# Attention and MLP in one program: turned weights regrouped within SBUF instead of through DRAM, turning placed behind scaling, and the first two MLP blocks spread up to slot 42

## Chip, cores and metric

One core of a Trainium2 chip. The metric is the device time of one execution in microseconds (us). Before the change the median was 1513.23 us of 3 runs (1508.47 to 1516.01).

## The reference

Thresholded attention over 8 batches and 8 heads, then an MLP with exact Gelu on the 4608 tokens that come out of it. All is float32.

```python
batch, n_heads, seq, head_dim = (8, 8, 576, 64)
scores = scale * np.matmul(q, k.transpose(0, 1, 3, 2))
thresh = np.max(scores, axis=-1, keepdims=True) - tau
scores = np.where(scores >= thresh, scores, -1000000000.0)
scores = scores - np.max(scores, axis=-1, keepdims=True)
attn = np.exp(scores)
attn = attn / (np.sum(attn, axis=-1, keepdims=True) + 1e-09)
x = np.matmul(attn, v)                    # (B,H,S,D), bridged to (B*S, H*D) = (4608, 512)
h = x @ w_in                              # d_ff = 2048
g = 0.5 * h * (1.0 + erf(h / sqrt(2)))
out = g @ w_out
```

## The kernel before

The program works on 32 head pairs (two heads of a batch), each in 5 slots: four of 128 queries and a tail of 64. Four pairs are a batch of 576 tokens. The first batch (slots 0 to 19) turns its attention weights with TensorE, while VectorE also converts the MLP weights. From the second batch on, VectorE turns blocks of 32x32 into `pd`, one buffer for each head, and DMA regroups `pd` into `pT`, the layout in which TensorE weighs `v`. `fill` strews MLP matmuls between the slots so that TensorE is never short of work. A block is the MLP of 256 tokens; a piece is one of 32 parts of the MLP weights, each converted by four VectorE instructions. A run is a stretch of contiguous bytes within a transfer; a transfer is issued when the queue takes it up and lands when its last byte is there.

```python
    pd = [const.tile([P, 4 * KR, P], FP32, name=f"pd{e}") for e in range(2)]        # one buffer for each head
    pd_tail = [const.tile([P, 4 * KR, Q], FP32, name=f"pd_tail{i}") for i in range(2)]
# ... cut ...
    def softmax_tail(p, i, early):
        # ... cut: masking (scalar_tensor_tensor on VectorE, reads the scores in PSUM), reciprocal ...
        for e in range(n):
            row = w[:, e * S:(e + 1) * S]
            if early:
                nc.scalar.activation(row, row, AF.Copy, bias=0.0, scale=rden[:, e:e + 1])
            else:
                nc.vector.tensor_scalar(row, row, rden[:, e:e + 1], None, op0=ALU.mult)

    def turn_p(p, i):
        s = st[p]
        w = s.pop(("p", i))
        n = 1 if i == NC else 2
        for e in range(n):
            to = pd_tail[p % 2] if i == NC else pd[e][:, :, i * Q:(i + 1) * Q]
            nc.vector.transpose(to[:, 0:NB, :], w[:, e * S:(e + 1) * S].rearrange("p (b i) -> p b i", i=Q))
        if i == NC - 1:
            s["turned"] = dram.tile([2, Q, 4 * KR, S], FP32, tag="turned", name="turned")
            for e in range(2):
                for a in range(4):
                    nc.sync.dma_start(s["turned"][e, :, :, a * P:(a + 1) * P], pd[e][a * Q:(a + 1) * Q])
        # ... cut: the tail, 4 transfers likewise from pd_tail ...

    def fetch_p(p):
        s = st[p]
        turned = s.pop("turned")
        s["pT"] = [one.tile([P, KR, S], FP32, tag=f"pT{e}", name=f"pT{e}") for e in range(2)]
        for e in range(2):
            nc.sync.dma_start(s["pT"][e], turned[e].rearrange("j (r k) s -> (j r) k s", k=KR))

    def weigh_v(p, h):
        # ... cut: 10 matmuls pT x v for one half (288 columns) of the queries, then ScalarE copies into x_blk ...

# ... cut ...
    for n in range(len(slots) + WEIGH + 1):          # a slot is 128 queries of both heads; slot 4 is the tail of 64
        p, i = divmod(n, SLOTS)
        batch = p // HP
        if p < NP:
            scores(p, i)                             # TensorE
            softmax_head(p, i)                       # row maxima on VectorE, Exp on ScalarE
        if 0 < p <= HP and i == 1:
            weigh_v(p - 1, 1)
            weighed = p
            if p == HP:
                convert(1e12)
                fill(BLK_NS / 2, 1)                  # half of the first MLP block
        if 0 < n <= len(slots):
            (turn_p if n > BATCH else turn_p_early)(*slots[n - 1])     # the slot before, ahead of masking
        if i == 0 and p > HP:
            fetch_p(p - 1)
        if p < NP:
            softmax_tail(p, i, batch < 2)
        # ... cut: loads, turning of q and k, weight conversion, fill() with MLP work ...
        if 0 < p <= HP and i == 0:
            weigh_v(p - 1, 0)
        elif p > HP and i == WEIGH:                  # WEIGH = 3
            for h in range(2):
                weigh_v(p - 1, h)
            weighed = p
```

## Time and profile before

| | before |
|---|---|
| time, median of 3 | 1513.23 us |
| TensorE busy, of the profiled 1511.5 us | 1440.8 us (95%) |
| VectorE busy | 901.7 us (60%) |
| scaling on ScalarE (second batch and first) | 72 instructions of 0.77 us mean |
| HBM traffic | 144.4 MB read, 92.0 MB written |

### The profile page before, as it was taken

Reading aid. Unit: us, or ns where it says so; the run is one execution under the profiler, and the core shown is the slowest. Engines: PE = TensorE matmul, PEld = TensorE weight load, DVE = VectorE, ACT = ScalarE, POOL = GpSimd, SP = SyncE. Lnnn points to the kernel's source line nnn. Section 1 sums busy time; section 2 is a strip of 40 time slices with the busy share of each in tenths; the row PEclk is TensorE's granted clock in tenths of the full one; section 3 lists DMA queues with packets and bytes.
Section 4 is the critical chain, followed back from the end, with each engine's and each line's share of the span. In section 5 each row is a group of like instructions: output and inputs, shape, how many; then the busy total and the mean of one; then the engine's idle time right before and its main releaser. Section 6 shows DMA issues by size and latency. Waiting matters only on the chain.

```text
span 1511.5 us, 17425 instructions
## 1 busy us (share of the span) xinstructions
PE 1440.8 (95%) x6092; PEld 897.7 (59%) x6092; DVE 901.7 (60%) x2089; ACT 635.4 (42%) x928; POOL 41.6 (3%) x84
## 2 busy tenths in 40 slices
PE   5877878899999999999999999999999999999998
PEld 4544635556565656666565656565757474765764
DVE  6998576676666766766766776666676675000000
ACT  5766344744444443535352535353535262110110
POOL 3221100000000000000000000000000000000000
PEclk9798989899999999999999999999999999999999
DMA  9876267767666667685767776666666655400000
GB/s 284 245 219 204 103 167 197 188 172 190 176 153 172 168 169 187 164 207 136 184 175 194 180 183 181 183 180 158 168 162 179 176 150 146 132 14 7 7 14 14
DMA packets 398887, 237.61 MB, mean 157 GB/s; under 512 B 230352, under 2 KB 380880, under 8 KB 391632
## 3 DMA queue, kind: packets, MB, share of 16 engines
q1 hardware_dynamic: 391632, 202.96, 52.1%
q0 software_dynamic: 7168, 33.54, 6.5%
q8 instruction: 49, 0.80, 0.2%
q14 instruction: 38, 0.31, 0.1%
HBM read 144.43 MB, written 92.01 MB: 156 GB/s over the span
## 4 chain that ended last, share of the span: by engine, by line
PE 83%; DVE 9%; ACT 3%; DMA 2%; SPq 2%; issue 1%; ACTq 0%; DVEq 0%
PE o_ps L437 32%; PE hT L426 31%; PE sc L320 11%; PE xT L398 9%; DVE p L345 3%; DVE nmx L331 2%; DVE power L174 1%; DMA turned<-pd 1%; ACT p L332 1%; DVE expo L165 1%; DVE w_in L176 1%; SPq L228 1%; DVE mant L172 1%; DMA pd<-in_moe_w_out_dram 1%; SPq L224 1%
## 5 line engine op out<-in xcount | busy, mean ns | idle before, releaser
L426 PE MATMUL hT<-x,w_in 128*128 128x256 f32 x2304 | 523.8, 385 | 4.0 <-ACT g L430 4.0
L437 PE MATMUL o_ps<-w_out,g 128*128 128x512 f32 x1152 | 516.1, 599 | 0.0
L426 PEld LDWEIGHTS hT<-x,w_in 128*128 128x128 f32 x2304 | 437.4, 192 | 92.2 <-issue 26.7
L331 DVE TENSOR_REDUCE nmx<-sc 128x1 f32<-128x576 f32 x288 | 206.3, 753 | 310.4 <-PE sc L320 309.5
L437 PEld LDWEIGHTS o_ps<-w_out,g 128*128 128x128 f32 x1152 | 215.1, 190 | 260.1 <-issue 257.1
L332 ACT ACTIVATE p<-sc,nmx 128x576 f32<-128x576 f32 x288 | 202.6, 741 | 335.2 <-DVE nmx L331 334.8
L345 DVE SCALAR_TENSOR_TENSOR p<-sc,thr,p 128x576 f32<-128x576 f32 x288 | 220.3, 797 | 14.0 <-ACT p L332 12.8
L320 PE MATMUL sc<-kT,qT 64*128 64x288 f32 x1024 | 185.7, 448 | 34.1 <-DVE p L345 33.6
L320 PEld LDWEIGHTS sc<-kT,qT 64*128 64x128 f32 x1024 | 102.8, 194 | 121.5 <-issue 103.8
L368 DVE STREAM_TRANSPOSE pd<-p 128x576 f32<-128x576 f32 x224 | 162.3, 757 | 14.2 <-DMA turned<-pd 14.1
L398 PE MATMUL xT<-pT,v 128*64 128x288 f32 x1280 | 164.9, 412 | 0.0
L430 ACT ACTIVATE g<-hT 128x512 f32<-128x512 f32 x144 | 85.2, 597 | 138.4 <-PE hT L426 137.7
L398 PEld LDWEIGHTS xT<-pT,v 128*64 128x64 f32 x1280 | 89.4, 138 | 75.3 <-issue 18.5
L356 DVE TENSOR_SCALAR p<-p,rden 128x576 f32<-128x576 f32 x216 | 103.7, 518 | 4.2
L430 ACT ACT_TABLE_LOAD x72 | 92.4, 1283 | 12.6 <-PE hT L426 11.6
L407 ACT COPY x<-xT 128x256 f32<-128x256 f32 (+7 forms) x128 | 29.3, 283 | 150.2 <-PE xT L398 150.2
L332 ACT ACT_TABLE_LOAD x71 | 91.1, 1283 | 2.8 <-DVE nmx L331 1.5
L440 ACT COPY o_sb<-o_ps 128x512 f32<-128x512 f32 x36 | 21.0, 584 | 147.6 <-PE o_ps L437 147.6
L354 ACT ACTIVATE p<-p,rden 128x576 f32<-128x576 f32 x72 | 52.3, 768 | 60.0 <-DVE rden L350 59.5
L320 PE MATMUL sc<-kT,q_tail 128*128 128x288 f32 x128 | 43.1, 462 | 18.7 <-DVE p L345 18.7
L320 PEld LDWEIGHTS sc<-kT,q_tail 128*128 128x128 f32 x128 | 23.3, 202 | 36.3 <-issue 32.4
L335 DVE TENSOR_SCALAR thr<-nmx,tau_eff 128x2 f32<-128x2 f32 (+1 forms) x160 | 36.2, 226 | 5.7
(65 smaller groups left out, 423.3 us busy)
## 6 DMA issues: line engine op xcount, KB each, us to landing
pT<-turned SPq DMA_DIRECT2D x56, 1440.0 KB, 8.1
turned<-pd SPq DMA_DIRECT2D x224, 320.0 KB, 5.2
out_dram<-o_sb SPq DMA_DIRECT2D x36, 256.0 KB, 2.2
turned<-pd_tail SPq DMA_DIRECT2D x112, 80.0 KB, 2.9
q<-in_q_dram SPq DMA_DIRECT2D x112, 72.0 KB, 8.9
k<-in_k_dram SPq DMA_DIRECT2D x112, 72.0 KB, 3.1
v<-in_v_dram SPq DMA_DIRECT2D x168, 40.0 KB, 2.2
raw<-in_moe_w_in_dram POOLq DMA_DIRECT2D x8, 512.0 KB, 7.9
```

The source lines that it names most:

```text
L320: nc.tensor.matmul(sc[e][:, h, 0:HALF], lhsT=lhsT, rhs=s["kT"][rows, at:at + HALF], start=True, stop=True)
L331: nc.vector.tensor_reduce(nmx[:, e:e + 1], sc, axis=AXIS.XY, op=ALU.max, negate=True)
L332: nc.scalar.activation(w[:, e * S:(e + 1) * S].rearrange("p (h s) -> p h s", h=2), sc, AF.Exp, bias=nmx[:, e:e + 1], scale=1.0)
L335: nc.vector.tensor_scalar(thr[:, 0:n], nmx[:, 0:n], -1.0, tau_eff, op0=ALU.mult, op1=ALU.subtract)
L345: nc.vector.scalar_tensor_tensor(row, sc[e][:, :, 0:HALF], thr[:, e:e + 1], row, op0=ALU.is_ge, op1=ALU.mult, accum_out=den[:, e:e + 1])
L354: nc.scalar.activation(row, row, AF.Copy, bias=0.0, scale=rden[:, e:e + 1])
L356: nc.vector.tensor_scalar(row, row, rden[:, e:e + 1], None, op0=ALU.mult)
L368: nc.vector.transpose(to[:, 0:NB, :], w[:, e * S:(e + 1) * S].rearrange("p (b i) -> p b i", i=Q))
L398: nc.tensor.matmul(xT[f, 0:HALF], lhsT=s["v"][:, e, c, :], rhs=pT[:, c, cols], start=(c == 0), stop=(c == KR - 1))
L426: nc.tensor.matmul(hT[:, j % 2, :], lhsT=w_in_sb[c][:, j * P:(j + 1) * P], rhs=x_blk[n][:, c, :], start=(c == 0), stop=(c == N_DM - 1))
L430: nc.scalar.activation(t, hT, AF.Gelu)
L437: nc.tensor.matmul(o[:, 0:d_model], lhsT=g[j][:, m * P:(m + 1) * P], rhs=w_out_sb[j], start=(j == 0), stop=(j == N_DF - 1))
```

## The change

Its intent: the regrouping goes straight from `pd` to `pT`, without the way through DRAM and the 56 reads back. Turning of a slot comes behind its own scaling, not ahead of the masking of the next slot, and scaling moves to VectorE one batch earlier. Two MLP blocks are spread evenly up to slot 42, with the first half of the first between the last weight conversions. For that, the weighing of the first batch is cut unevenly (columns 0 to 256 at slot 2 of the same pair, 256 to 576 at slot 0 of the next). Cut to its core:

```diff
-    dram = ctx.enter_context(tc.tile_pool(name="dram", bufs=2, space=bass.MemoryType.DRAM))
...
-    EARLY_PIECES = 24
+    EARLY_PIECES = 22
...
-            nc.gpsimd.memset(t, 0.0)
+            nc.gpsimd.memset(t[:, :, NB - 3 * KR:KR, :], 0.0)
...
         if i == NC - 1:
-            s["turned"] = dram.tile([2, Q, 4 * KR, S], FP32, tag="turned", name="turned")
+            s["pT"] = [one.tile([P, KR, S], FP32, tag=f"pT{e}", name=f"pT{e}") for e in range(2)]
             for e in range(2):
                 for a in range(4):
-                    nc.sync.dma_start(s["turned"][e, :, :, a * P:(a + 1) * P], pd[e][a * Q:(a + 1) * Q])
+                    regroup(s["pT"][e], a * P, P, pd[e], a)
...   (the tail likewise; fetch_p goes)
+    def regroup(to, at, n, src, a):
+        nc.sync.dma_start(to[:, :, at:at + n], src[a * Q:(a + 1) * Q])
 
-    def weigh_v(p, h):
+    def weigh_v(p, lo, hi):
...   (columns lo to hi in place of a half)
-    WEIGH = 3
-
-    goal = [0.0] + [1.5 + 2.08 * i for i in range(B - 1)]
+    WEIGH = 2
+    FIRST = BLK_NS / 2
+    SECOND = 2 * BLK_NS - FIRST
+
+    goal = [0.0] + [1.9 + 2.03 * i for i in range(B - 1)]
...
+        early = batch == 0
...
-        if 0 < p <= HP and i == 1:
-            weigh_v(p - 1, 1)
-            weighed = p
+        if 0 < p <= HP and i == 0:
+            turn_p_early(p - 1, NC)
+            weigh_v(p - 1, TOK, S)
             if p == HP:
-                convert(1e12)
-                fill(BLK_NS / 2, 1)
-        if 0 < n <= len(slots):
-            (turn_p if n > BATCH else turn_p_early)(*slots[n - 1])
-        if i == 0 and p > HP:
-            fetch_p(p - 1)
+                tokens = S
+        if early and i:
+            turn_p_early(p, i - 1)
         if p < NP:
-            softmax_tail(p, i, batch < 2)
+            softmax_tail(p, i, early)
+        if n == BATCH:
+            for _ in range(len(pieces) - EARLY_PIECES):
+                convert(2100)
+                fill(FIRST / (len(pieces) - EARLY_PIECES), tokens)
+            convert(1e12)
+        if HP <= p < NP:
+            turn_p(p, i)
...
+            if n <= 2 * BATCH + WEIGH:
+                share = SECOND / (BATCH + WEIGH)
+            fill(share, tokens)
+        if early and i == 2:
+            weigh_v(p, 0, TOK)
+            if p == HP - 1:
+                tokens = TOK
         elif p > HP and i == WEIGH:
             for h in range(2):
-                weigh_v(p - 1, h)
-            weighed = p
+                weigh_v(p - 1, h * HALF, (h + 1) * HALF)
+            if p % HP == 0:
+                tokens = batch * S
```

More of the change, by code (lines that the diff above doesn't have):

```diff
@@ L376, in turn_p @@
                 e, at = divmod(a * Q, TAIL)
-                nc.sync.dma_start(
-                    s["turned"][e, :, :, MAIN + at:MAIN + at + Q], pd_tail[p % 2][a * Q:(a + 1) * Q])
-    def fetch_p(p):
-        s = st[p]
-        turned = s.pop("turned")
-        s["pT"] = [one.tile([P, KR, S], FP32, tag=f"pT{e}", name=f"pT{e}") for e in range(2)]
-        for e in range(2):
-            nc.sync.dma_start(s["pT"][e], turned[e].rearrange("j (r k) s -> (j r) k s", k=KR))
-    def weigh_v(p, h):
+                regroup(s["pT"][e], MAIN + at, Q, pd_tail[p % 2], a)
+    def regroup(to, at, n, src, a):
+        nc.sync.dma_start(to[:, :, at:at + n], src[a * Q:(a + 1) * Q])
+    def weigh_v(p, lo, hi):
         b, hp = divmod(p, HP)
         s = st[p]
-        cols = slice(h * HALF, (h + 1) * HALF)
         xT = ps.tile([P, 512], FP32, tag="mm", name="xT")
@@ L398, in weigh_v @@
                 nc.tensor.matmul(
-                    xT[f, 0:HALF], lhsT=s["v"][:, e, c, :], rhs=pT[:, c, cols],
+                    xT[f, 0:hi - lo], lhsT=s["v"][:, e, c, :], rhs=pT[:, c, lo:hi],
                     start=(c == 0), stop=(c == KR - 1))
-        at = lo = b * S + h * HALF
-        while at < lo + HALF:
-            n, o = divmod(at, TOK)
-            size = min(TOK - o, lo + HALF - at)
+        at = lo
+        while at < hi:
+            n, o = divmod(b * S + at, TOK)
+            size = min(TOK - o, hi - at)
             if n not in x_blk:
@@ L408, in weigh_v @@
             at += size
-        if h:
+        if hi == S:
             del st[p]
@@ L444, with fill @@
     mlp = {"n": 0, "steps": None, "next": None, "debt": 0.0}
-    def fill(ns, batches):
+    def fill(ns, tokens):
         mlp["debt"] += ns
@@ L451, in fill @@
                 n = mlp["n"]
-                if n == N_BLK or (n + 1) * TOK > batches * S:
+                if n == N_BLK or (n + 1) * TOK > tokens:
                     break
@@ L470 @@
     BATCH = HP * SLOTS
-    WEIGH = 3
-    goal = [0.0] + [1.5 + 2.08 * i for i in range(B - 1)]
-    weighed = 0
+    WEIGH = 2
+    FIRST = BLK_NS / 2
+    SECOND = 2 * BLK_NS - FIRST
+    goal = [0.0] + [1.9 + 2.03 * i for i in range(B - 1)]
+    tokens = 0
     for n in range(len(slots) + WEIGH + 1):
@@ L497 @@
             (turn_qk if p + 1 >= HP else turn_qk_early)(p + 1)
-        if batch == 0:
+        if early:
             convert(EARLY_PIECES * 2100 / BATCH)
-        elif n > BATCH + 1:
+        elif n > BATCH:
             done = min(batch, B - 1)
             share = (goal[done] - goal[done - 1]) * BLK_NS / BATCH
-            if batch == 1:
-                share = (goal[1] - 0.5) * BLK_NS / (BATCH - 2)
-            fill(share, weighed // HP)
-        if 0 < p <= HP and i == 0:
-            weigh_v(p - 1, 0)
+            if n <= 2 * BATCH + WEIGH:
[5 more added lines that the diff above has]
+                tokens = TOK
         elif p > HP and i == WEIGH:
             for h in range(2):
-                weigh_v(p - 1, h)
-            weighed = p
+                weigh_v(p - 1, h * HALF, (h + 1) * HALF)
+            if p % HP == 0:
+                tokens = batch * S
     convert(1e12)
-    fill(1e12, B)
+    fill(1e12, B * S)
 _INS = ["q", "k", "v", "tau", "moe_w_in", "moe_w_out"]
```

## The prediction

> **What bounds the kernel now.** I read the page first (busy shares, slices), then a table of engine times by stretch, then the waits between 181 and 330 us, then the instructions around the idle stretches and the DMA queue's own line. From the page:
>
> ```profile
> PE 1440.8 (95%) x6092; PEld 897.7 (59%) x6092; DVE 901.7 (60%) x2089; ACT 635.4 (42%) x928; POOL 41.6 (3%) x84
> ...
> PE   5877878899999999999999999999999999999998
> DVE  6998576676666766766766776666676675000000
> ...
> PEclk9798989899999999999999999999999999999999
> ```
>
> TensorE is busy 95% of the span, and from the ninth slice on in full. All that can be won is in the first 330 us (a slice is 37.8 us). The table by stretch (length, then busy time of PE, PEld, DVE, ACT, POOL, then clock):
>
> ```profile
> 0.00:230.00 230.00, 174.52 (x784) 110.69 (x786) 182.30 (x438) 131.80 (x225) 41.57 (x84) 0.88 0.69 202
> ...
> 330.00:1310.00 980.00, 980.00 (x4287) 606.91 (x4287) 656.83 (x1509) 423.58 (x588) 0.00 (x0) 1.00 0.67 175
> ...
> 137.00:148.00 11.00, 8.80 (x59) 4.90 (x59) 10.18 (x28) 6.27 (x12) 1.22 (x3) 1.00 0.51 184
> 148.00:181.50 33.50, 29.94 (x132) 25.38 (x130) 18.94 (x37) 10.49 (x17) 5.49 (x10) 0.95 0.37 134
> 181.50:313.00 131.50, 111.61 (x441) 65.23 (x440) 85.61 (x195) 75.80 (x106) 0.00 (x0) 0.90 0.63 160
> ```
>
> Three stages. Up to 148 us (first batch) VectorE is the bound: 18 to 19 of every 20 us between 20 and 160. From 148 to 181.5 TensorE runs half of the first MLP block while VectorE converts the last 8 weight pieces. From 181.5 to 313 (second batch) nobody is full: PE has 19.9 us idle and a clock of 0.90. After 330 there is nothing but TensorE work, and it is the same work after the change.
>
> What holds PE in the third stage, by the waits (total, times, longest) and two places in the order of time:
>
> ```profile
> PE sc L320 <- DVE p L345: 19.6, 11, 5.8
> DVE pd L368 <- DMA turned<-pd: 11.7, 4, 4.6
> DVE p L345 <- ACT p L332: 9.5, 7, 1.9
> ...
> 249.12 0.78 DVE L368 STREAM_TRANSPOSE pd<-p 128x576 f32<-128x576 f32 x1 [4.63 <-DMA turned<-pd]
> ...
> 250.76 2.99 PE L320 MATMUL sc<-kT,qT 64*128 64x288 f32 x8 [4.65 <-DVE p L345]
> ```
>
> The scores of a slot wait for the masking (L345) of the slot before, which frees their PSUM. The masking stands behind the turning (L368) in VectorE's order, and the turning waits until the DMA has emptied `pd`. So a 4.6 us DMA wait becomes 4.65 us of idle PE, and the next scores take 2.99 us instead of 1.24. The third line is ScalarE: in this batch it scales (1.44 us) as well as Exp and Gelu with two table loads of 1.28 us a slot, and Exp comes late.
>
> The DMA queue over one head pair, with the issue time of each group:
>
> ```profile
> 234.42 10.68 SPq L373 DMA_DIRECT2D turned<-pd  x8
> 245.19 4.36 SPq L377 DMA_DIRECT2D turned<-pd_tail  x4
> 250.07 1.55 SPq L386 DMA_DIRECT2D pT<-turned  x2
> ```
>
> `pd` is free 14.7 us after its first transfer is issued (234.42 to 249.12); at 632.83 to 647.38 it is 14.5 us again.
>
> **What the Trainium skill says.** "TensorE: Matmul & The Clock Gate", Part 1, says that the clock falls to half after an idle window of about 3.4 us and needs as much work to recover. The trace agrees in kind: after 5.77 us idle at 213.8 the scores took 2.99 us instead of 1.24. "ScalarE: Activation LUTs", What ACT_TABLE_LOAD costs, gives 1283 ns for a load; the trace has the same 1283. "DMA: Bandwidth & Descriptors", Why small descriptors are slow, says that transfers within SBUF do not suffer the penalty of small descriptors that HBM has; no transfer of that kind is in this trace, and I use it only for a lean towards a shorter regroup.
>
> **The change part by part.**
>
> *Regrouping within SBUF.* Per head pair the 12 transfers out of `pd` stay, with the same 512 and 128 byte runs; their target becomes `pT`. The two 1440 KB reads per pair (56 of them, 8.1 us to landing) and their waits on the queue go. In the steady part this is hidden: PE has no idle there and the weights are needed about 29 us after the turning. `pT` has one buffer, but its last reader (weighing at slot 2) stands before the scores of slot 3 on PE, so the transfer after slot 3's turning finds it free. Gain after 330 us: 0.
>
> *Two pieces fewer in the first batch.* A piece is 4 VectorE instructions, 2.0 us (146.79 to 148.79). Two, while VectorE is the bound: 4.1 us earlier at slot 20.
>
> *The MLP start.* Before, PE did the scores of slot 20 at 137.2, both halves of weighing, the scores of slot 21, and began the half block at 148.1; it took 14.08 + 15.77 us with 3.56 us idle between, because the Gelus stood behind all conversions on ScalarE. Now the second part of weighing (columns 256 to 576) follows the copies of `pT`, which ended at 142.7, less 4.1 = 138.6; 3 us for it; half block from 141.6; Gelus and conversions alternate, so no stall: 29.9 us, end at 171.5. Before: 181.5. 10.0 us earlier, but the scores of one more slot (1.2 us) are left to do.
>
> *The second batch.* PE work at undisturbed durations: scores 1.2 a slot, weighing 5.0 a pair, a block 128 x 0.226 + 64 x 0.449 = 57.7. Before, 181.5 to 313: 18 slots 21.6 + 3 weighings 15 + one block 57.7 = 94.3 of 131.5; lost 37 us (20 idle, the rest slow clock). Now 171.5 to slot 43: 22 slots 26.4 + 4 weighings 20 + 1.5 blocks 86.6 = 133.0, plus a loss.
> The loss: scaling moves to VectorE, 0.52 per head half. A full slot there is then reductions and threshold 1.57, masking and reciprocal 1.96, scaling 1.0, turning 1.43 = 6.0; a pair is 4 x 6.0 + 4.0 (tail) + 2.6 (turning q, k) = 30.6 us. PE per pair: 5 x (1.2 + 3.94) + 5.0 = 30.7. Both are full, so jitter costs; I put 1.5 us a pair. `pd` is wanted again about 10.4 us after its first transfer (turning of slot 3 to turning of the next slot 0), against 12.5 to 14.5 needed (less if transfers within SBUF are faster): 1 to 3 us of stall a pair. It no longer stands ahead of the masking, so PE pays only what exceeds the fill. With about 1 us a pair of slow clock: 4 to 5 us a pair, 4.4 pairs, 20 (range 8 to 32).
>
> *Sum at the same state.* Before at 313 us had 3 scores, 1 weighing and half a block less done than slot 43 now: 3.6 + 5.0 + 28.9 = 37.5, so before stands there at 350.5. Now: 171.5 + 133 + 20 = 324.5. Gain 26. Weighing earlier and in unequal parts in the first batch may delay scores by up to 2 us in all; the smaller memset (POOL, 0.67 us x 4) is off the path. Net 25 to 26, so 1513 - 26 = 1487.
>
> **The rivals.**
> 1. *The second batch becomes full of PE work.* If transfers within SBUF run faster than those to DRAM, `pd` is free in under 10.4 us, the stalls vanish and the loss falls to 8: gain 36 to 38, about 1476. For it: the queue issues the first of 8 transfers in 0.56 us and the later ones in 1.42 (back pressure, so speed decides). Against it: the packets are as many and as small.
> 2. *VectorE becomes the bound of the second batch.* 30.6 us a pair of work, in order, with Exp behind Gelu and table loads. If it loses 3 us a pair more, the loss is 32: about 1499.
> 3. *The transfer wait moves, not goes.* The queue needs 10.5 + 4.4 + some 15 us of loads a pair, 30 of 31; if transfers within SBUF are slower than those to DRAM, turning waits more, and the weighing (some 20 us after turning in this batch) too. About 1500, and in the steady part slots of 7 us still hide it.
> 4. *DMA was the thing.* Someone who reads 238 MB and 0.67 DMA share as the bound would expect much; PE busy 980.00 of 980 speaks against it.
>
> **Range and chances.** 2% is 30.3 us, i.e. 1483. Fixed part 9 us from the earlier MLP start, 17 +- 11 from the second batch. Range 1474 to 1501. Faster by over 2%: 0.36. Within: 0.62. Slower: 0.02, since no PE work is added and the part after 330 us has slack everywhere.
>
> **What would show it.** PE busy stays near 1430 to 1440 with PE work the same, the tail after attention unchanged; the half block begins near 142 and runs in one piece; PE idle between 172 and 325 falls from 20 to about 10 and the clock rises to about 0.95; ScalarE's scaling count falls from 72 to 36; DMA bytes fall by 83 MB read. Wrong would be: `pd` waits of over 4 us a pair still turning into PE idle, weighing waiting for `pT`, PE below full after 330 us, or a first batch that does not get shorter.

## More of the kernel before

What matters later are four more lines of the page. The first is the share of each engine in the chain that ended last; the second is the turning into `pd` (count, then busy time and mean ns, then idle time ahead of it and what ended it); the last two are transfers (count, KB each, median us from issue to landing).

```profile
PE 83%; DVE 9%; ACT 3%; DMA 2%; SPq 2%; issue 1%; ACTq 0%; DVEq 0%
...
L368 DVE STREAM_TRANSPOSE pd<-p 128x576 f32<-128x576 f32 x224 | 162.3, 757 | 14.2 <-DMA turned<-pd 14.1
...
pT<-turned SPq DMA_DIRECT2D x56, 1440.0 KB, 8.1
turned<-pd SPq DMA_DIRECT2D x224, 320.0 KB, 5.2
```

Turning waited 14.1 us for DMA in the whole execution.

## The result, and the profile after

The changed kernel took 1534.76 us (median of 4 runs, 1531.32 to 1537.37) against 1513.70 us of the kernel before in the same rounds (1508.47 to 1516.01). Ratios here are the mean time of one kernel's fast runs over that of the other's of the same rounds, so not quite the ratio of the medians: 1.0143, 95% interval 1.0106 to 1.0179. It is slower by 1.4%, where 1487 us and at most 1501 were forecast. The result is correct.

From the page of the changed kernel (busy time of each engine; then the slices of 38.2 us; then HBM traffic, the chain's shares, turning and its transfer):

```profile
PE 1453.2 (95%) x6092; PEld 912.9 (60%) x6092; DVE 928.7 (61%) x2125; ACT 605.8 (40%) x886; POOL 40.1 (3%) x84
...
PE   6778977889999999999999999999999999999999
...
PEclk8777998899999999999999999999999999999999
...
HBM read 61.85 MB, written 9.44 MB: 47 GB/s over the span
...
PE 77%; DVE 11%; SPq 6%; DMA 5%; ACT 1%; issue 1%; DVEq 0%; ACTq 0%
...
L367 DVE STREAM_TRANSPOSE pd<-p 128x576 f32<-128x576 f32 x224 | 163.7, 760 | 112.3 <-DMA pT<-pd 111.1
...
pT<-pd SPq DMA_DIRECT2D x224, 320.0 KB, 6.0
```

HBM traffic fell as intended: 144.4 MB read became 61.9. But turning now waits 111.1 us for DMA instead of 14.1, and DMA with its queue (SPq) makes 11% of the chain that ended last, from 4%. TensorE is busy 12.4 us more with the same 6092 matmuls: a matmul group that waits in its middle, or runs at a lower clock, counts as busy. By stretch (length; busy time of PE, PEld, DVE, ACT, POOL; clock; DMA share; GB/s), and last the second batch of before:

```profile
0.00:137.00 137.00, 101.97 (x474) 67.48 (x474) 110.16 (x280) 87.33 (x155) 30.61 (x66) 0.79 0.74 222
137.00:172.00 35.00, 32.86 (x138) 26.40 (x138) 30.55 (x66) 16.33 (x27) 9.44 (x18) 0.80 0.77 272
172.00:330.00 158.00, 133.61 (x536) 78.83 (x536) 112.94 (x255) 58.66 (x82) 0.00 (x0) 0.91 0.42 83
330.00:1310.00 980.00, 969.01 (x4186) 600.54 (x4185) 675.07 (x1527) 419.90 (x581) 0.00 (x0) 0.99 0.51 102
...
172.00:330.00 158.00, 137.90 (x538) 81.06 (x536) 97.72 (x224) 83.67 (x116) 0.00 (x0) 0.91 0.61 153
```

The fourth line is the surprise: between 330 and 1310 us, where before had TensorE busy for 980.00 of 980 at clock 1.00, it now lacks 11 us and some clock. And the second batch (172 to 330) is no fuller than it was: TensorE is busy 133.61 us against 137.90, both at clock 0.91.

The waits of that steady stretch (total, times, longest):

```profile
DVE pd L367 <- DMA pT<-pd: 90.2, 25, 5.8
```

Before had 2.4 us there. Two places in the order of time, one in the second batch and one in the steady part (start, duration, what; in brackets the idle time ahead and what ended it):

```profile
200.68 12.84 SPq L379 DMA_DIRECT2D pT<-pd  x8
...
211.04 0.78 DVE L367 STREAM_TRANSPOSE pd<-p 128x576 f32<-128x576 f32 x1 [1.17 <-DMA pT<-pd]
...
218.03 0.78 DVE L367 STREAM_TRANSPOSE pd<-p 128x576 f32<-128x576 f32 x1 [6.22 <-DMA pT<-pd]
...
221.46 3.00 PE L319 MATMUL sc<-kT,qT 64*128 64x288 f32 x8 [7.14 <-DVE p L344]
...
603.32 12.70 SPq L379 DMA_DIRECT2D pT<-pd  x8
...
620.42 0.78 DVE L367 STREAM_TRANSPOSE pd<-p 128x576 f32<-128x576 f32 x1 [3.60 <-DMA pT<-pd]
...
624.08 1.71 PE L319 MATMUL sc<-kT,qT 64*128 64x288 f32 x8
```

The eight transfers are issued over 12.84 us, head 0 first. The turning of the next pair's slot 0 for head 1 needs the last of them landed: it starts 17.4 us after the first issue (200.68 to 218.03), 17.1 us in the steady part. Before it was 14.5 to 14.7. The stall of 6.22 us on VectorE becomes 7.14 us of idle TensorE, and the scores behind it run at 3.00 us instead of 1.24. In the steady part no idle time is shown ahead of the scores at 624.08, but the group takes 1.71 us: the wait is hidden inside a busy group.

### The profile page after: what moved, and what is told of

It is laid out like the page before. It is cut to its first block, busy times and chain, and to the rows that moved or that the text cites. A ratio compares the mean times of both kernels' runs of the same rounds, so it can differ in the third digit from the quotient of the medians.

```text
span 1529.5 us, 17324 instructions
## 1 busy us (share of the span) xinstructions
PE 1453.2 (95%) x6092; PEld 912.9 (60%) x6092; DVE 928.7 (61%) x2125; ACT 605.8 (40%) x886; POOL 40.1 (3%) x84
## 4 chain that ended last, share of the span: by engine, by line
PE 77%; DVE 11%; SPq 6%; DMA 5%; ACT 1%; issue 1%; DVEq 0%; ACTq 0%
PE hT L418 31%; PE o_ps L429 24%; PE xT L390 11%; PE sc L319 10%; SPq L379 5%; DMA pT<-pd 4%; DVE nmx L330 3%; DVE p L344 3%; DVE pd L367 1%; DVE power L173 1%; DVE p L355 1%; ACT p L331 1%; DVE thr L334 0%; DVE w_in L175 0%; ACT p L353 0%
## 5 line engine op out<-in xcount | busy, mean ns | idle before, releaser
L418 PE MATMUL hT<-x,w_in 128*128 128x256 f32 x2304 | 517.3, 382 | 0.0
L344 DVE SCALAR_TENSOR_TENSOR p<-sc,thr,p 128x576 f32<-128x576 f32 x288 | 225.3, 816 | 32.1 <-ACT p L331 18.9
L319 PE MATMUL sc<-kT,qT 64*128 64x288 f32 x1024 | 196.1, 453 | 46.9 <-DVE p L344 46.2
L367 DVE STREAM_TRANSPOSE pd<-p 128x576 f32<-128x576 f32 x224 | 163.7, 760 | 112.3 <-DMA pT<-pd 111.1
L319 PEld LDWEIGHTS sc<-kT,qT 64*128 64x128 f32 x1024 | 107.6, 196 | 139.1 <-issue 121.0
L390 PE MATMUL xT<-pT,v 128*64 128x288 f32 (+2 forms) x1280 | 175.0, 428 | 6.4 <-DVE pT L278 4.9
L390 PEld LDWEIGHTS xT<-pT,v 128*64 128x64 f32 x1280 | 100.0, 143 | 81.8 <-issue 15.2
L355 DVE TENSOR_SCALAR p<-p,rden 128x576 f32<-128x576 f32 x252 | 121.0, 518 | 4.9
L399 ACT COPY x<-xT 128x64 f32<-128x64 f32 (+7 forms) x124 | 29.2, 286 | 160.7 <-PE xT L390 160.7
L319 PE MATMUL sc<-kT,q_tail 128*128 128x288 f32 x128 | 37.7, 418 | 9.2 <-DVE p L344 9.2
L319 PEld LDWEIGHTS sc<-kT,q_tail 128*128 128x128 f32 x128 | 24.4, 194 | 21.3 <-issue 16.8
L273 PE MATMUL tr<-ident,p 128*128 128x128 f32 x144 | 29.2, 359 | 2.2 <-ACT p L353 2.0
```

The lines of the kernel that those rows point to most:

```text
L319: nc.tensor.matmul(sc[e][:, h, 0:HALF], lhsT=lhsT, rhs=s["kT"][rows, at:at + HALF], start=True, stop=True)
L344: nc.vector.scalar_tensor_tensor(row, sc[e][:, :, 0:HALF], thr[:, e:e + 1], row, op0=ALU.is_ge, op1=ALU.mult, accum_out=den[:, e:e + 1])
L390: nc.tensor.matmul(xT[f, 0:hi - lo], lhsT=s["v"][:, e, c, :], rhs=pT[:, c, lo:hi], start=(c == 0), stop=(c == KR - 1))
L418: nc.tensor.matmul(hT[:, j % 2, :], lhsT=w_in_sb[c][:, j * P:(j + 1) * P], rhs=x_blk[n][:, c, :], start=(c == 0), stop=(c == N_DM - 1))
```

## The experiments

Fourteen kernels ran, all correct, in the order of their letters; here they are grouped by question. The time of before in the same rounds was 1510.66 to 1512.6 us (medians of 7 runs). Each has 4 timed runs.

| kernel | median us | ratio to before, 95% interval |
|---|---|---|
| changed kernel | 1534.76 | 1.0143 [1.0106, 1.0179] |
| a1: changed, regroup through DRAM | 1502.30 | 0.9939 [0.9906, 0.9972] |
| a2: before, regroup within SBUF | 1558.54 | 1.0308 [1.0282, 1.0335] |
| a3: changed, old early weighing | 1524.51 | 1.0084 [1.0063, 1.0105] |
| a4: changed, runs of 1280 bytes | 1506.34 | 0.9955 [0.9927, 0.9983] |
| b1: a1 and a3 | 1494.45 | 0.9877 [0.9848, 0.9906] |
| b2: a4 and old early weighing | 1492.14 | 0.9863 [0.9844, 0.9881] |
| b3: b2, each half sent when turned | 1470.27 | 0.9719 [0.9699, 0.9740] |
| b4: b1 with turning at its old place | 1502.08 | 0.9934 [0.9913, 0.9955] |
| c1: changed, second early part later | 1533.82 | 1.0150 [1.0128, 1.0172] |
| c2: changed, transfers cut in halves (256 bytes) | 1484.12 | 0.9811 [0.9777, 0.9846] |
| d1: c2 and old early weighing | 1468.43 | 0.9724 [0.9700, 0.9748] |
| d2: b1, transfers cut in halves | 1484.93 | 0.9839 [0.9816, 0.9862] |
| d3: c2, halves interleaved | 1522.40 | 1.0086 [1.0065, 1.0107] |
| d4: changed, first early part later | 1537.21 | 1.0172 [1.0149, 1.0194] |

### Is it the regrouping? a1 and a2

The first theory: transfers within SBUF are slower than those to DRAM, and the wait for `pd` costs most of the loss. The rival: the new places of turning and weighing do it. a1 puts the way through DRAM back into the changed kernel:

```diff
-            s["pT"] = [one.tile([P, KR, S], FP32, tag=f"pT{e}", name=f"pT{e}") for e in range(2)]
+            s["turned"] = dram.tile([2, Q, 4 * KR, S], FP32, tag="turned", name="turned")
...
-                    regroup(s["pT"][e], a * P, P, pd[e], a)
+                    regroup(s["turned"][e], a * P, P, pd[e], a)
...
-    WEIGH = 2
+    WEIGH = 3
...   (the tail likewise)
+        if i == 0 and p > HP:
+            fetch_p(p - 1)
```

> The changed kernel with only the regroup put back through DRAM (weights written to DRAM, read back at slot 0 of the next pair, weighing at slot 3 instead of 2, everything else as changed). Theory T (transfers within SBUF are slower than those to DRAM, 17.2 against 14.5 us until pd is free, and the turning now waits for it): pd free again in about 14.5 us, waits of the turning on DMA fall from 111 us to below 60, time falls to about 1515 to 1522. Rival R1 (the regroup is beside the point, the early weighing order costs all 18 us): stays at 1530 to 1536.

a2 does the opposite, the new regroup alone in the kernel before:

```diff
-                    nc.sync.dma_start(s["turned"][e, :, :, a * P:(a + 1) * P], pd[e][a * Q:(a + 1) * Q])
+                    nc.sync.dma_start(s["pT"][e][:, :, a * P:(a + 1) * P], pd[e][a * Q:(a + 1) * Q])
...   (the tail likewise; fetch_p goes)
```

> The kernel before with only the regroup moved into SBUF (its schedule, its weighing at slot 3, its turning one slot later kept). Theory T: pd free after 17 us instead of 14.5, turning stands before the masking, so each pair of the second batch loses 2 to 3 us more and the steady part shows some idle: 1520 to 1535. Rival R1 (schedule alone is at fault): 1508 to 1514, as before or a little better for the reads gone.

a1 took 1502.30 us, 32 less than the changed kernel; a2 took 1558.54, 47 more than before. Both went further than their forecasts. By a2 the regroup within SBUF alone costs more than the whole loss. In a1's order of time (same columns), first in the second batch, then in the steady part:

```profile
209.18 10.37 SPq L380 DMA_DIRECT2D turned<-pd  x8
...
223.97 0.78 DVE L368 STREAM_TRANSPOSE pd<-p 128x576 f32<-128x576 f32 x1 [4.53 <-DMA turned<-pd]
...
638.38 1.43 DVE L368 STREAM_TRANSPOSE pd<-p 128x576 f32<-128x576 f32 x2
```

The same eight transfers of 512 byte runs go out in 10.37 us instead of 12.84, and `pd` is free after 14.8 us. Waits of turning on DMA in the whole execution: 11.9 us against 111.1; in a2 78.5 us, and TensorE's scores wait for masking 76.4 us against 52.3 in before.

One thing more than the regroup differs in a1, as its forecast says: weighing is at slot 3 instead of 2. There it stands behind the turning of slot 3 (its 5.07 us begin at 621.13, that turning at 620.43), so `pd` is wanted again only after 17.9 us in the steady part, against 13.6 in the changed kernel (a table below shows how these are read). That is why the turning at 638.38 shows no wait. The 14.4 us that DRAM needs would have missed 13.6; the 17.2 us within SBUF would have met 17.9 (though within SBUF, with one buffer of `pT`, the transfer would first have to wait for that weighing). So the 32 us of a1 belong to the regroup and the place of weighing together, and how they divide was not run. a2 is free of this: its `pd` is wanted after 11.6 us in the second batch and 14.8 in the steady part, before's after 11.7 and 14.8, and it is free after 16.9 and 17.1 instead of 14.4. That the regroup within SBUF is the larger cause is shown by a2. Why it is slow was not yet.

### Why is it slow? Run length, or how pd is freed: a4, c2, d3

Second theory: the number of runs sets the duration. a4 lays `pd` and `pT` out so that a transfer moves runs of 1280 bytes (5 blocks of 64 columns):

```diff
-    pd = [const.tile([P, 4 * KR, P], FP32, name=f"pd{e}") for e in range(2)]
+    pd = [const.tile([P, 2, 4 * KR, 64], FP32, name=f"pd{e}") for e in range(2)]
...
-            s["pT"] = [one.tile([P, KR, S], FP32, tag=f"pT{e}", name=f"pT{e}") for e in range(2)]
+            s["pT"] = [one.tile([P, S // 64, KR, 64], FP32, tag=f"pT{e}", name=f"pT{e}") for e in range(2)]
             for e in range(2):
                 for a in range(4):
-                    regroup(s["pT"][e], a * P, P, pd[e], a)
+                    for h in range(2):
+                        nc.sync.dma_start(
+                            s["pT"][e][:, 2 * a + h].rearrange("p k x -> p (k x)"),
+                            pd[e][a * Q:(a + 1) * Q, h].rearrange("j b x -> j (b x)"))
...   (all that writes or reads pd and pT follows the layout)
```

> The changed kernel with pT and pd laid out in groups of 64 columns, so that the main regroup within SBUF moves the same bytes in runs of 1280 bytes instead of 512 (16 transfers of 128 runs instead of 8 of 640). If the cost is per run: the issue of the main regroup falls from 12.7 to 6 to 9 us, pd is free in 9 to 13 us, the waits of the turning all but vanish, time 1505 to 1515. If the cost is per byte[...]: pd stays at 16 to 18 us and the time at 1530 to 1537.

1506.34 us, 28 less than the changed kernel, with 14.6 us of waits of turning. It looked like the proof. c2 then doubled the suspected cost, the number of runs, with the layout left alone:

```diff
-                for a in range(4):
-                    regroup(s["pT"][e], a * P, P, pd[e], a)
+                for h in range(2):
+                    for a in range(4):
+                        nc.sync.dma_start(
+                            s["pT"][e][:, :, a * P + h * D:a * P + (h + 1) * D],
+                            pd[e][a * Q:(a + 1) * Q, :, h * D:(h + 1) * D])
```

> The changed kernel with each of the 8 main regrouping transfers cut in two of half the columns: the same bytes, 256 byte runs in place of 512, twice as many runs. If the transfers within SBUF are bound by bytes alone (32 partitions at one end), pd is free after about 17.5 us as before, and the time stays at 1535 +- 5. If the number of runs counts too (with 1280 byte runs it was 14.1 us): from 17.5 for 10240 runs and 14.1 for 4096 a straight line gives 0.55 us per 1000 runs, so about 23 us for 20480 runs, turning stalls some 5 us more a pair, and the time is 1570 to 1640.

Both forecasts of this run failed. With twice as many runs the kernel took 1484.12 us, 50 less than the changed kernel. In the steady part of c2:

```profile
605.87 18.57 SPq L373 DMA_DIRECT2D pT<-pd  x16
611.70 1.43 DVE L367 STREAM_TRANSPOSE pd<-p 128x576 f32<-128x576 f32 x2
...
625.20 1.43 DVE L367 STREAM_TRANSPOSE pd<-p 128x576 f32<-128x576 f32 x2
```

The queue starts at 605.87, ahead of the turning of slot 3 at 611.70: the first four transfers need only what slots 0 and 1 turned, and go as soon as the weighing of the pair before (600.77 to 605.84) has read `pT` for the last time. And the turning of the next slot 0 (625.20, both heads in one piece) shows no wait, since it needs only half 0 of `pd`, while half 1 of head 1 may still be on its way. Turning's waits on DMA in the whole execution: 0.6 us. So c2 had changed two things beside the run length: the size of what is waited for, and when the first part may start. d3 keeps the short runs and their number and only puts the two halves of each partition group one after the other:

```diff
-                for h in range(2):
-                    for a in range(4):
+                for a in range(4):
+                    for h in range(2):
```

> The run with short runs (1484.1 us), with only the order of its 16 transfers altered: both halves of a partition group one after the other, so that half 0 of the second head is complete with the 15th transfer and only one transfer can start early. If the freeing of half 0 is what gave the 50 us, the waits of turning come back: 80 to 110 us of them, 1525 to 1540 us. If smaller transfers or more in flight are faster by themselves: 1484 +- 5.

1522.40 us, a little below the forecast: most of the waits are back. In its order of time:

```profile
595.78 20.68 SPq L373 DMA_DIRECT2D pT<-pd  x16
601.62 1.43 DVE L367 STREAM_TRANSPOSE pd<-p 128x576 f32<-128x576 f32 x2
...
618.63 0.78 DVE L367 STREAM_TRANSPOSE pd<-p 128x576 f32<-128x576 f32 x1 [2.68 <-DMA pT<-pd]
```

Now only one transfer goes out ahead of slot 3, and half 0 of head 1 is complete with the 15th of 16. In all 72.3 us of waits on DMA, in 21 times, and 16.7 us more in five waits for which the profile names no releaser. So the order of the very same transfers decides 38 of the 50 us. This is shown. The remaining 12 between d3 and the changed kernel are not taken apart.

The landings in the kept traces show why. Counted from the end of the turning of slot 3 for head 0, two times matter for each pair: when the last transfer has landed that the turning of the next slot 0 for head 1 must wait for ("free"), and when that turning would have begun if neither head had waited ("wanted"). Medians, second batch and then steady part:

| | free after, us | wanted after, us | waits of turning, us |
|---|---|---|---|
| before | 14.4, 14.4 | 11.7, 14.8 | 14.1 |
| a2 | 16.9, 17.1 | 11.6, 14.8 | 78.5 |
| a1 | 14.7, 14.4 | 12.6, 17.9 | 11.9 |
| changed | 17.1, 17.2 | 10.1, 13.6 | 111.1 |
| d3 | 16.1, 16.3 | 10.0, 13.6 | 72.3 (and 16.7) |
| a4 | 13.4, 13.3 | 10.0, 13.5 | 14.6 |
| c2 | 10.1, 10.0 | 10.0, 13.5 | 0.6 |

Each kernel's waits follow from which of its wanted times it misses: the changed kernel and d3 miss both, a4 that of the second batch alone, c2 neither by more than 0.1 us. The change made `pd` wanted earlier, too: 10.1 and 13.6 us against 11.7 and 14.8 in before. Of the 2.8 us by which the regroup within SBUF is longer than that to DRAM, 1.9 lie before the first landing (5.3 us after its issue, against 3.4); why, no run shows.

Run length has a share of its own, though: a4 also frees `pd` in halves, and a4 and d3 send the halves in the same order and depend on them in the same way, and 1280 against 256 bytes makes 1506.34 out of 1522.40. The next group shows when that counts.

### What is left once pd comes free in halves? b2, b3, d1, d2

b3 was run before c2, on the way to a version that beats both. It starts from b2 (long runs, old early weighing) and sends half 0 at slot 2:

```diff
+        if HP <= p < NP and i == 2:
+            send_half(p, 0)          # after the weighing of the pair before, in program order
...
-            for e in range(2):
-                for a in range(4):
-                    for h in range(2):   # ...
+            send_half(p, 1)          # at slot 3
```

> Regroup within SBUF in runs of 1280 bytes (as a4) and the first batch's weighing at the old slots (256 and 320 columns at slots 0 and 1 of the next pair). If costs add: 1506 - 10 = about 1496. If it beats b1 by more than 5 us, transfers within SBUF are worth having once their runs are long.

> b2 with the main regroup sent in two parts: columns of slots 0 and 1 after slot 2, those of slots 2 and 3 after slot 3, so that pd's first half is empty long before the next pair. If the wait for pd is what is left between b2 and full use of TensorE in the second batch (a4: 13 us of PE waiting on masking from 180 to 330 us): the waits of the turning on DMA go to under 3 us and the time falls 5 to 10 us below b2, to 1486 to 1491. If not: within 3 us of b2.

b2 took 1492.14 us with 14.0 us of waits of turning, only 2 less than b1, so by its own forecast long runs alone do not make transfers within SBUF worth having. b3 took 1470.27 with no such wait: 22 us for sending the first half earlier, where 5 to 10 were forecast. In b3 TensorE was busy 157.76 of the 160 us from 180 to 340, at clock 1.00; in b2 144.81 at 0.91.

d1 is c2, short runs in halves, with the old early weighing (the edit of a3 below):

> The run with short runs (each main transfer cut in two column halves, 1484.1 us) with the weighing of the first batch at its old places. The short runs did not slow the kernel as the count of runs would have it; they took 50 us off. New theory: what costs in the changed kernel is that pd is freed as a whole; with halves the first four transfers start before the turning of slot 3, and the turning of the next slot 0 waits for half 0 alone. The old places of weighing gave 10 to 14 us three times, so 1470 to 1476 if the two add, equal to the 1470.3 of long runs sent in two parts, which would make the run length worth nothing once the halves are apart. If long runs are worth something by themselves: 1478 to 1485.

1468.43 us, just under the forecast and within the noise of b3. So no worth of long runs is left once the halves are apart; they had only brought the regroup below the time at which `pd` is wanted again in the steady part. The new layout of `pd` and `pT` was not needed. Its stretches:

```profile
172.00:330.00 158.00, 155.75 (x674) 92.82 (x673) 140.42 (x321) 73.43 (x102) 0.00 (x0) 1.00 0.65 123
330.00:1310.00 980.00, 980.00 (x4261) 611.28 (x4260) 645.29 (x1455) 410.62 (x572) 0.00 (x0) 1.00 0.50 96
```

The second batch holds 155.75 us of TensorE work at full clock in 158 us, and the steady part is full again.

d2 asks whether transfers within SBUF are then worth anything. It is b1, through DRAM, with the same cut in halves.

```diff
-                for a in range(4):
-                    regroup(s["turned"][e], a * P, P, pd[e], a)
+                for h in range(2):
+                    for a in range(4):
+                        nc.sync.dma_start(
+                            s["turned"][e, :, :, a * P + h * D:a * P + (h + 1) * D],
+                            pd[e][a * Q:(a + 1) * Q, :, h * D:(h + 1) * D])
```

> The run with the regroup through DRAM and old weighing (1494.5 us) with the 8 transfers from pd to DRAM cut in two column halves. If freeing pd in halves is what matters, the last waits of turning (12.3 us in 5) go as well, and the time is 1476 to 1488, so that transfers within SBUF are worth little for the time at all. If runs of 256 bytes to DRAM are slow, as the skill page on descriptors says for HBM (below 512 bytes), issue takes 15 to 20 us instead of 10.4 for the 16, and the time is 1495 to 1530.

1484.93 us, 10 less than b1 and 16.5 more than d1. So, with `pd` freed in halves, going within SBUF is worth 16.5 us, together with the weighing at slot 2 instead of 3 that goes with it: the intent of the change holds, under a condition that the change did not meet. d2 still has 6.4 us of waits of turning and its second batch less TensorE work:

```profile
172.00:330.00 158.00, 147.81 (x608) 83.44 (x608) 134.07 (x306) 67.43 (x95) 0.00 (x0) 0.97 0.74 182
```

Which of its waits make up the 16.5 us was not tested. A second pair of `pd` buffers would free turning altogether; it does not fit (a build of it stopped for lack of SBUF: one pool needs 22 KB per partition where 4.16 KB are left), so that stays untried.

### The first batch: a3, c1, d4

a3 puts the early weighing back to its old places and halves, and leaves all else of the change:

```diff
-            weigh_v(p - 1, TOK, S)
             if p == HP:
+                weigh_v(p - 1, 0, HALF)
+                weigh_v(p - 1, HALF, S)
                 tokens = S
+        if 0 < p < HP and i == 1:
+            weigh_v(p - 1, HALF, S)
...
-        if early and i == 2:
-            weigh_v(p, 0, TOK)
-            if p == HP - 1:
-                tokens = TOK
+        if early:
+            if p and i == 0:
+                weigh_v(p - 1, 0, HALF)
```

> The changed kernel with only the weighing of the first batch put back to the old places (both halves of 288 after the pair, at slots 0 and 1 of the next). Theory W (in the first batch the larger second part of weighing at slot 0 and the first part at slot 2 hold up the scores of the next slot, 9 us in all): the half block of the MLP starts at about 143 to 146 instead of 151.4, time 1523 to 1528. Rival R2 (the slip in the first batch is given back because the second batch is bound by the transfers anyway): 1531 to 1536. If both T and W hold, a1 and a3 together account for about 25 us.

1524.51 us, 10 less. The same step gave 14 us between a4 and b2, 16 between c2 and d1 and 8 between a1 and b1 (below). Where it lies: the scores of the tail slots, once a pair, in the changed kernel

```profile
34.65 2.26 PE L319 MATMUL sc<-kT,q_tail 128*128 128x288 f32 x4 [2.08 <-DVE p L344]
...
135.94 1.21 PE L319 MATMUL sc<-kT,q_tail 128*128 128x288 f32 x4 [2.45 <-DVE p L344]
...
146.24 5.26 PE L390 MATMUL xT<-pT,v 128*64 128x320 f32 x20 [0.69 <-DVE pT L278]
151.43 27.89 PE L418 MATMUL hT<-x,w_in 128*128 128x256 f32 x128
```

and in a3:

```profile
37.22 1.79 PE L319 MATMUL sc<-kT,q_tail 128*128 128x288 f32 x4 [2.64 <-DVE p L344]
...
130.09 2.26 PE L319 MATMUL sc<-kT,q_tail 128*128 128x288 f32 x4 [4.87 <-DVE p L344]
...
144.59 27.89 PE L418 MATMUL hT<-x,w_in 128*128 128x256 f32 x128
```

Three pairs take 101.3 us in the changed kernel, 33.8 each, and 92.9 in a3, 31.0 each; before had (131.85 - 34.66) / 3 = 32.4 with two conversions more. The uneven weighing costs 2.8 us a pair, and the half block starts 6.8 us later although the change was to make it start earlier. Two more runs moved one part alone. c1, the larger part one slot later:

```diff
-            weigh_v(p - 1, TOK, S)
             if p == HP:
+                weigh_v(p - 1, TOK, S)
                 tokens = S
+        if 0 < p < HP and i == 1:
+            weigh_v(p - 1, TOK, S)
```

> The changed kernel with one thing altered: in the first batch the larger second part of the weighing (columns 256 to 576) goes from slot 0 of the next head pair to its slot 1, behind the scores of slot 1; the first part stays at slot 2. The run with both parts at their old places took 1524.5 us against 1534.8, 10 us less. If the larger part at slot 0, waiting for the copies of pT ahead of the next scores, is what costs: most of it comes back, 1525 to 1528 us, and the scores of slot 20 begin near 137 us instead of 142. If the first part at slot 2 costs: 1532 to 1536, as the changed kernel.

d4, the smaller part later, to the end of slot 0 of the next pair:

```diff
             if p == HP:
+                weigh_v(p - 1, 0, TOK)
...
-        if early and i == 2:
-            weigh_v(p, 0, TOK)
+        if early and p and i == 0:
+            weigh_v(p - 1, 0, TOK)
```

> The changed kernel with the first part of the weighing of the first batch (columns 0 to 256) moved from slot 2 of the same head pair to the end of slot 0 of the next; the larger part stays ahead of it at slot 0. With the larger part alone moved the time did not change (1533.8 against 1534.8), with both moved it was 1524.5. If the first part at slot 2 is what costs: 1522 to 1527. If it takes both at old places: 1531 to 1537.

1533.82 and 1537.21 us: neither alone brings anything. c1 by itself pointed at the smaller part, and d4 refuted that. In the profiled runs a pair took 32.6 us in c1 and 34.8 in d4, so each part at its new place keeps the pair above the 31.0 of a3; c1 also started its first pair 6 us later than the changed kernel (40.52 against 34.65), behind a late load of k. That the placement costs about 10 us is shown; how the two parts share it stays open.

### What remains of the change: b1 and b4

b1 has both suspects undone (a1 and a3 together): what is left is turning behind scaling, scaling on VectorE one batch earlier, two pieces fewer, and the spread of the blocks.

> The changed kernel with both suspects undone: regroup through DRAM (weighing at slot 3) and the first batch's weighing in its old places. What stays of the change: turning behind scaling, scaling on VectorE from the second batch on, 22 early pieces, two blocks spread to slot 42. If the two costs are separate they add up: 1502 - 10 = about 1492 (1488 to 1497), near the 1487 forecast for the whole change, which would make the rest of that forecast right. If the weighing was only a cost where the second batch was bound by transfers: 1499 to 1504.

1494.45 us. The two parts add up: 32.5 and 10.3 taken off alone, 40.3 together. b4 also puts turning back to its old place, one slot later, ahead of the masking:

```diff
+        if BATCH < n <= len(slots):
+            turn_p(*slots[n - 1])
+        if i == 0 and p > HP:
+            fetch_p(p - 1)
         if p < NP:
             softmax_tail(p, i, early)
...
-        if i == 0 and p > HP:
-            fetch_p(p - 1)
-        if HP <= p < NP:
-            turn_p(p, i)
```

> b1 with the turning put back one slot later, ahead of the masking, where a wait of the turning for pd holds up the masking and so the next scores. If turning behind scaling is worth something with DRAM regroup (my forecast: pd waits no longer stand ahead of the masking): 3 to 10 us slower than b1. If it is worth nothing: within 2 us of b1.

1502.08 us: turning behind scaling is worth 8 us where the regroup goes through DRAM. Not all of that need be the masking: turning waits 18.5 us in b4 against 12.3 in b1, since `pd` is wanted after 10.5 us in its second batch instead of 11.8. The two were not separated. In the second batch of b4 (172 to 330) TensorE was busy 138.25 us at clock 0.92, in b1 143.01 at 0.96.

## Why the prediction was wrong

**The step that failed.** The prediction counted "1 to 3 us of stall a pair" in the second batch, from "10.4 us" wanted and "12.5 to 14.5 needed (less if transfers within SBUF are faster)". The wanted time was about right (10.1). The needed time was the mis-sized term: in the four pairs of the second batch it measured 16.8 to 18.0 us, and the stalls 5.8 to 6.8 us for head 1, with 0.8 to 1.2 more for head 0. The lean to a shorter regroup pointed the wrong way: in the steady part the eight transfers took 17.1 us from the first issue to the last landing within SBUF, and 14.3 us to DRAM in before and in a1 (medians).

**The step behind it.** "It no longer stands ahead of the masking, so PE pays only what exceeds the fill" failed too. Turning of a slot still stands ahead of the reductions and the masking of the next one in VectorE's order, and TensorE's fill of that slot was used up: stalls of 6.22 and 6.77 us became 7.14 and 8.32 us of idle TensorE. Moving the turning was right (8 us by b4), but it did not keep a wait of 6 to 7 us inside turning away from TensorE.

**"Gain after 330 us: 0".** As a loss this was not weighed at all: the argument was that nothing would be lost, since the weights are needed much later. That is true of the weights; it overlooked that `pd` itself is wanted again, after 14.8 us in before, which 14.4 just met, and after 13.6 in the changed kernel, which 17.2 missed. The forecast never worked out this time for the steady part. Rival 3 named the mechanism, "turning waits more", and dismissed it for the steady part with "slots of 7 us still hide it". There the waits were 90.2 us in 25 times; TensorE lacked 11 us and ran at 0.99. Weighing busy time by clock (an estimate; the clock is rounded), the changed kernel is short of c2 by 155.2 - 121.6 = 34 us of work between 172 and 330 and 980 - 959 = 21 us between 330 and 1310, and ahead by 6 us before 172. That is 48; the two profiled spans differ by 44.1. So the miss lies in both stages.

**The early weighing.** "May delay scores by up to 2 us in all" measured about 8.4 us over three pairs, and 8 to 16 us of time in four comparisons. So the half block, forecast from 141.6 to 171.5, ran from 151.4 to 179.3: 2 us ahead of the old 181.5, not 10.

**What held.** The half block ran in one piece of 27.89 us, where before had 14.08 and 15.77 with 3.56 idle between. DMA read 82.6 MB less (forecast 83). Scaling on ScalarE fell from 72 to 36 instructions, and turning behind scaling gained 8 us (b4). TensorE stayed the engine that sets the time. The forecast of 1487 us for the whole is met within 8 us by b1, which leaves out the two parts that were mis-sized; that it comes near is no proof of its terms, since b1 has neither the regroup nor the early weighing that the sum was made for. And rival 1, the second batch becoming full, "about 1476", is what d1 and b3 show (1468 and 1470), by freeing `pd` in halves and by the old early weighing, not by faster transfers.

**My theory during the study.** After a4 I held that the number of runs made the transfers slow. c2 refuted it, 86 us below the lowest time that theory had forecast. One run that improves does not show why it improved: a4 had changed more than the run length (its 16 transfers also free `pd` in halves), and the cost that it removed could be removed otherwise.

## What to carry to other kernels

A buffer that is emptied by DMA and refilled by an engine has a deadline: compare the time from its first transfer's issue to the last landing with the time until it is wanted again, for every stage, and include what stands behind the refilling engine. When a transfer is a little too slow for its deadline, first look at what is waited for: the same bytes in the same number of pieces, ordered so that the part wanted first is sent first, was worth 38 us, more than a faster layout. And a wait that the profile shows as nearly nothing says nothing of the margin: some 2.7 us more for the regroup turned 14.1 us of waits into 78.5 (a2), and with `pd` wanted 1.2 to 1.6 us earlier into 111.1 (the changed kernel).

## What the Trainium skill lacked or had wrong

- "DMA: Bandwidth & Descriptors", Why small descriptors are slow (HBM only), says that transfers within SBUF do not suffer from small descriptors. Here they did, somewhat: from the first to the last landing of transfers queued one behind the other (medians of 23 pairs of the steady part, read from the landings in the traces), bytes moved at 166 (d3) and 177 GB/s (c2) in runs of 256 bytes, 194 (changed) in 512, and 201 (a4) in 1280. Nor must it be read as "within SBUF is faster than to DRAM": in runs of 512 bytes it was 210 GB/s to DRAM (before).
- The same page and section puts the penalty on HBM, and its Specifications give 512 bytes as the least for line rate. In the direction SBUF to DRAM little of this showed: 201 GB/s in runs of 256 bytes (d2), 211 in 512 (a1), read in the same way.
- No page says how a wait inside a group of matmuls looks in a profile: here the group counts as busy, 1.71 us instead of 1.24 for eight matmuls, and TensorE's busy time rose by 12.4 us with the same number of matmuls, in part through the lower clock.
